# Windowed attention with a two-layer FFN, one core: the last six token chunks go through the first FFN product in pairs, by seven half-size products whose weights stream from a DRAM scratch

## The chip, the core and the metric

The kernel runs on one NeuronCore of a Trainium2 chip. Times are device microseconds (us) of one launch. TensorE is called PE (its weight loads PEld), VectorE DVE, ScalarE ACT, GpSimd POOL; SP is the queue that issues the DMAs.

## What is computed

Attention with 8 heads of width 64 over 8 sequences of 576 tokens, then, with the heads joined to 512 numbers per token, a feed-forward layer on the 4608 tokens; `window` is 32, `dilation` 4, `w_in` is 512 x 2048 and `w_out` 2048 x 512:

```python
scores = scale * np.matmul(q, k.transpose(0, 1, 3, 2))
mask_plain = (rel >= 0) & (rel < window)
mask_dil = (rel >= 0) & (rel < window * dilation) & (rel % dilation == 0)
masks = np.stack([mask_plain if h < H // 2 else mask_dil for h in range(H)], axis=0)
scores = np.where(masks[None, :, :, :], scores, -1000000000.0)
...
return np.matmul(attn, v).astype(np.float32)
...
h = x @ w_in
inv_sqrt2 = np.float32(1.0 / np.sqrt(2.0))
g = 0.5 * h * (1.0 + erf(h * inv_sqrt2))
return (g @ w_out).astype(np.float32)
```

## The kernel before, in words

The 4608 tokens are nine chunks of 512. Each operand of the FFN is split into a high and a low part of type fp32r, and a product of two such operands is three matmuls: high by high, low by high, high by low. One matmul is 128x128 weights by 512 tokens.

The feed-forward work of a chunk is 16 blocks `f` of 128 hidden units. For one `f`, `ffn_h` (line 551, matmuls at line 543) does 4 x 3 = 12 matmuls into one of PSUM's banks 4 and 5, ACT makes the GELU (line 557) and rounds it to the high part (line 560), and DVE subtracts to get the low part (line 562). `ffn_o` (line 564, matmuls at 567) then does 12 matmuls for the same `f` into the four output banks 0 to 3. So a chunk has 192 matmuls of the first product (h) and 192 of the second (o). Chunks 1 to 8 run them as eight h blocks, eight o blocks, eight h blocks and eight o blocks; in the last of these stages each output bank takes its 24 matmuls in one go and is copied out (line 585).

All 16 weight blocks stay in SBUF from chunk 0 on, as `weight` tiles of one pool, `wpool`, which has 19 buffers of 1 MB; the other three hold q, k and v as they arrive.

The attention of chunk n+1 is interleaved with the FFN of chunk n: scores (`scores`, line 372, 64 matmuls for two head pairs), the masked minimum (`lowest`, lines 406 and 412, DVE), the exponentials (`softmax`, line 420, ACT: eight per head pair), the reciprocal and the scaling (lines 429, 431, 445, DVE), the transposes (`turn`, lines 458 and 463, DVE), the product with v (`av`, line 507) and the split of its result into the x tiles (`xout`, lines 530 and 533).

Chunk 0, with the load and split of the weights and the attention of chunks 0 and 1, is laid out by a planner (`Plan`) with costs and ranks. From chunk 1 on the order is written by hand: each step gets a position in units of FFN blocks (`add`, `upto`), and is emitted when the FFN loop has come there. Every engine works its own instructions in the order of the program.

## Time and profile before

| | us |
|---|---|
| three timed runs, median | 896.36 |
| lowest and highest of them | 893.29, 896.65 |
| span of the profiled execution | 892.8 |
| PE busy in it | 878.7 |
| ACT busy | 387.2 |
| DVE busy | 354.0 |

The profile is of one further execution; its span runs from the first to the last instruction, and that is the time that its views divide up. A row of a group gives line, engine, operation, tiles and shape, the count, then busy time and the mean of one in ns, then the idle time in front of the group and what ended it. The chain of waits lists what the end of the span hung on, piece by piece, as start, length, engine and line. In the table of stretches each engine's busy time stands with its instruction count, then the granted TensorE clock as a share, the busy share of the 16 DMA engines and the GB/s.

### The profile page before, as it was taken

The numbers are of one execution on the slowest core, as the hardware profiler recorded it, in microseconds if no ns is written. First come the engines' busy times: TensorE is split into PE (matmuls) and PEld (weight loads), VectorE is DVE, ScalarE is ACT, GpSimd is POOL, SyncE is SP. The second block draws the span as 40 slices with busy tenths as digits, with TensorE's granted clock in tenths as the row PEclk, the third lists the DMA queues.
The fourth block names the chain that finished last, engine by engine and source line by source line (L and its number), as shares of the span: only waits on it lengthen the run. The fifth ranks groups of instructions, "written<-read, shape, count | busy, mean of one in ns | idle before, by whom it ended". The sixth has DMA issues, their size and how long they took to land.

```text
span 892.8 us, 19041 instructions
## 1 busy us (share of the span) xinstructions
PE 878.7 (98%) x8403; PEld 723.5 (81%) x8403; DVE 354.0 (40%) x594; ACT 387.2 (43%) x1028; POOL 11.6 (1%) x45
## 2 busy tenths in 40 slices
PE   6999999999999999999999999999999999999998
PEld 5778888888888888888888888888888888888886
DVE  6896963622254214621462136222542164212020
ACT  6886833733273325442354237332723263414040
POOL 5000000000000000000000000000000000000000
PEclk8899999999999999999999999999999999999999
DMA  9966124003300240004100330033002330010001
GB/s 373 415 253 235 48 95 143 1 1 119 120 1 1 68 150 23 0 1 173 65 1 1 131 107 1 1 119 120 1 1 72 126 124 0 1 38 12 1 1 47
DMA packets 16212, 71.20 MB, mean 80 GB/s; under 512 B 1794, under 2 KB 2050, under 8 KB 11650
## 3 DMA queue, kind: packets, MB, share of 16 engines
q1 hardware_dynamic: 16130, 70.00, 21.2%
q8 instruction: 65, 1.06, 0.5%
q14 instruction: 17, 0.14, 0.0%
HBM read 60.55 MB, written 9.44 MB: 78 GB/s over the span
## 4 chain that ended last, share of the span: by engine, by line
PE 95%; ACT 3%; DMA 1%; issue 1%; SPq 0%; DVE 0%; ACTq 0%
PE ps L567 44%; PE ps L543 43%; PE ps L507 3%; PE ps L372 3%; DMA raw_qk<-qk 1%; PE ps L486 1%; PE ps L719 1%; ACT sm L420 1%; PE ps L471 1%; PE ps L499 0%; ACT sm L442 0%; ACT raw_w L266 0%; ACT weight L297 0%; ACT L557 0%; ACT gf L557 0%
## 5 line engine op out<-in xcount | busy, mean ns | idle before, releaser
L567 PE MATMUL ps<-g,weight 128*128 128x512 f32 x1728 | 402.5, 391 | 0.5 <-DVE g L562 0.5
L543 PE MATMUL ps<-x,weight 128*128 128x512 f32 x1728 | 401.4, 390 | 0.0
L543 PEld LDWEIGHTS ps<-x,weight 128*128 128x128 f32 x1728 | 322.9, 188 | 68.0
L567 PEld LDWEIGHTS ps<-g,weight 128*128 128x128 f32 x1728 | 322.8, 188 | 68.2 <-DVE g L562 1.0
L562 DVE TENSOR_TENSOR g<-gf,g 128x512 fp32r<-128x512 f32 x144 | 99.6, 692 | 384.7 <-ACT g L560 384.7
L557 ACT ACTIVATE gf<-ps 128x512 f32<-128x512 f32 x144 | 86.2, 599 | 316.6 <-PE ps L543 316.6
L560 ACT CAST g<-gf 128x512 fp32r<-128x512 f32 x144 | 89.4, 621 | 4.6
L420 ACT ACTIVATE sm<-sm,st 128x64 f32<-128x64 f32 (+1 forms) x224 | 74.9, 337 | 0.1
L196 ACT COPY o_sb<-ps 128x512 f32<-128x512 f32 (+1 forms) x35 | 20.3, 581 | 108.7 <-PE ps L567 103.2
L533 DVE TENSOR_TENSOR x<-ps,x 128x512 fp32r<-128x512 f32 (+1 forms) x38 | 32.0, 847 | 88.4 <-ACT x L530 88.4
L530 ACT CAST x<-ps 128x512 fp32r<-128x512 f32 (+1 forms) x38 | 29.9, 798 | 64.0 <-PE ps L507 40.6
L463 DVE STREAM_TRANSPOSE turned<-sm 32x256 f32<-32x256 f32 x104 | 45.4, 436 | 2.0
L420 ACT ACTIVATION_READ_ACCUMULATOR sm<-sm,st 128x1 f32 x224 | 42.1, 188 | 0.0
L372 PEld LDWEIGHTS ps<-raw_qk 64*32 64x32 f32 x2304 | 25.0, 108 | 9.2 <-issue 5.2
L372 PE MATMUL ps<-raw_qk 64*32 64x64 f32 (+1 forms) x2304 | 28.8, 232 | 2.8 <-DMA raw_qk<-qk 2.7
L507 PEld LDWEIGHTS ps<-turned,v_sb 64*64 64x64 f32 x1664 | 25.4, 135 | 4.6 <-issue 4.6
L507 PE MATMUL ps<-turned,v_sb 64*64 64x32 f32 x1664 | 26.9, 220 | 0.0
L420 ACT ACTIVATE sm<-ps,st 128x64 f32<-128x64 f32 x64 | 19.0, 328 | 6.0 <-DVE st L431 3.6
L445 DVE TENSOR_TENSOR sm<-sm,st 128x512 f32<-128x512 f32 x30 | 20.8, 692 | 0.9
L292 DVE SCALAR_TENSOR_TENSOR weight<-raw_w,spare 128x1024 fp32r<-128x1024 uint32 x16 | 19.6, 1224 | 0.5
L286 DVE SCALAR_TENSOR_TENSOR raw_w<-raw_w,spare 128x1024 uint32<-128x1024 uint32 x16 | 19.5, 1218 | 0.1
L297 ACT CAST weight<-raw_w 128x1024 fp32r<-128x1024 f32 x16 | 18.5, 1156 | 1.2 <-DVE raw_w L286 1.2
(58 smaller groups left out, 269.5 us busy)
## 6 DMA issues: line engine op xcount, KB each, us to landing
v_sb<-v SPq DMA_DIRECT2D x17, 1024.0 KB, 5.2
raw_qk<-qk SPq DMA_DIRECT2D x32, 512.0 KB, 5.2
raw_w<-w SPq DMA_DIRECT2D x16, 1024.0 KB, 14.0
outT<-o_sb SPq DMA_DIRECT2D x35, 256.0 KB, 2.2
mid_w<-w SPq DMA_DIRECT2D x4, 1023.5 KB, 16.6
raw_qk<-qk_ld SPq DMA_DIRECT2D x2, 1024.0 KB, 7.0
v_wide<-v_ld SPq DMA_DIRECT2D x2, 768.0 KB, 5.6
raw_qk<-qk_lp SPq DMA_DIRECT2D x2, 640.0 KB, 4.0
```

Of the source, the lines that this page charges most:

```text
L372: nc.tensor.matmul(s.sc[32 * r:32 * r + 32, h, c0:c0 + s.nk], x[:, q0:q0 + 32], x[:, k0:k0 + s.nk], start=s.c > 1, stop=s.c > 1 or u == NU ...
L420: nc.scalar.activation(t, s.sc[:, i // NU, at:at + 2 * KB] if s.c < 2 else t, AF.Exp, bias=s.st[:, 0, i:i + 1], scale=SCALE if s.c < 2 els ...
L445: nc.vector.tensor_mul(s.all, s.all, t.unsqueeze(2).broadcast_to((P, 2 * NU, 2 * KB)))
L463: nc.vector.transpose(s.t[32 * to:32 * to + 32, :, r % 2], s.all[32 * r:32 * r + 32, :, j * KB:(j + 1) * KB])
L507: nc.tensor.matmul(px(r)[h * D:(h + 1) * D, u * KB:(u + 1) * KB], s.v[rows, u, j, h * D:(h + 1) * D], s.t[rows, h * NU + slot(s, u), j], s ...
L530: nc.scalar.copy(h, y)
L533: nc.vector.tensor_sub(l, y, h)
L543: nc.tensor.matmul(bank, weights[f][:, t, cc * P:(cc + 1) * P], x[:, xx], start=n == 0, stop=n == 3 * NC - 1)
L557: nc.scalar.activation(gf, bank, AF.Gelu)
L560: nc.scalar.copy(g[:, 0], gf)
L562: nc.vector.tensor_sub(g[:, 1], gf, g[:, 0])
L567: nc.tensor.matmul(ps[:, d], weights[f][:, t, DM + d * P:DM + (d + 1) * P], gs[f][:, u], start=f == 0 and n == 0, stop=f == NF - 1 and n == 2)
```

## The change

Chunk 0 stays as it is. Chunks 1 and 2 keep the direct product (`chunk`). Chunks 3 to 8 are taken as three pairs. For a pair, the 1024 tokens are cut into two halves of 512 (alternate runs of 32 tokens), the 512 inputs of the FFN into two halves of 256, and the 2048 hidden units into `f` and `f + 8`. The four quarter products of that 2x2 block form are got from seven products P1 to P7 of half size, each 6 matmuls for one `f` of 8 (`product`), and their sums. So the first product of a pair is 7 x 6 x 8 = 336 matmuls in place of 384. The second product stays direct, 2 x 192.

What that needs beside the matmuls:

- **Weights and sums of weights** (`prepare`, in chunk 1, eight times, one every 6.5 us of the plan): POOL adds high and low part of two weight blocks (2 x 512 columns), DVE makes four sums or differences, ACT and DVE split five of the results into high and low parts in the four slots of a tile `units`, and SP stores them in a DRAM scratch: five stores of 256 KB from `units` (line 817), two of 256 KB (lines 821, 822) and two of 512 KB (line 825) straight from the `weight` tiles. Eight times that is 72 stores.
- **Streaming back** (`fetch`, line 1070): the weight blocks leave SBUF in chunk 2; their buffers become a ring of six, two tiles of x (`late["x", ..]`) and eight tiles `c` that hold the four quarter products of one `f` in fp32. Per pair 8 + 8 + 16 blocks of 1 MB, 768 KB and 1 MB come through the ring.
- **Operands** (`operand`): sums of x halves on DVE, split by ACT and DVE into `xs` tiles, seven per pair of two tiles each, in place of the x tiles of `xout`; `put_x` (line 892) now only copies a chunk's x from PSUM.
- **Adding up**: per pair and `f` three copies from PSUM to `c` by ACT (`set_to`) and six adds of a PSUM bank to a part of `c` by DVE (`add_up`, line 1153).
- **GELU** on the sums in `c` in SBUF (line 1214), five blocks ahead of the second product (`LEAD`), where before it read PSUM.

All work from chunk 1 on stands in one list of events with planned times (0.2267 us for a matmul, `MM`), sorted; attention is planned by `duo` (two head pairs), uses PSUM banks 6 and 7 alone, and the other six banks are handed out in the order in which they were given back (`free`). A pair has three stages: x (P1, P2, P4, P7: 24 matmuls per `f`), z (P3, P5, P6: 18 per `f`), and the two second products (2 x 192). The attention of the next two chunks lies in them. `softmax` may now be interrupted between its eight exponentials. The host undoes the order of the tokens at the end.

The core of the diff:

```diff
-    for c in range(1, NCH):
-        for f in range(half):
-            at_once(ffn_h(c, f, gs))
-            upto(base + f + 1)
...
+    def prepare(t, f):
...
+        def sums(i):
+            def go():
+                st["p"] = have("prep", lambda: kept([P, 4, 2, NW1], F32, "prep"))
+                x = weights[f + HALF * i][:, :, 0:DM].bitcast(F32)
+                nc.gpsimd.tensor_add(st["p"][:, i].rearrange("p k n -> p (k n)"), x[:, 0], x[:, 1])
...
+        def unit(n, of, to):
+            def high():
+                q = have("units", lambda: kept([P, 4, 2, NW1], F32R, "units"))
+                nc.scalar.copy(q[:, n % 4, 0], st["p"][:, of[0], of[1]])
+            def low():
+                q = late["units"]
+                nc.vector.tensor_sub(q[:, n % 4, 1], st["p"][:, of[0], of[1]], q[:, n % 4, 0])
+            def put():
+                nc.sync.dma_start(to, late["units"][:, n % 4].bitcast(F32))
+        def plain():
+            nc.sync.dma_start(wx[f][:, P2], b(0).bitcast(F32))
+            nc.sync.dma_start(wz[f][:, P5], b(3).bitcast(F32))
+            for i in range(2):
+                g = f + HALF * i
+                nc.sync.dma_start(w2[g // 2][:, g % 2], weights[g][:, :, DM:].bitcast(F32))
+        ev(t - 2, 4, sums(0))
+        ev(t - .9, 4, sums(1))
+        ev(t - 1.2, 0, plain)
+        for n, (of, to) in enumerate(targets):
+            at = t + 1.1 * n
+            if n == 0 or first[n] != first[n - 1]:
+                ev(at, 4, both(first[n]))
+            high, low, put = unit(5 * f + n, of, to)
+            ev(at + .5, 4, high)
+            ev(at + 1, 4, low)
+            ev(at + 1.5, 0, put)
...
+        for f in range(HALF + 1):
+            w = lambda f=f: slab_w(first + f, 4)
+            if f < HALF:
+                t = unit(t, ops, ("x", P1), f, w)
+                ev(t, .5, set_to(f, X22, (("x", P1), f), True))
+                t = unit(t, ops, ("x", P4), f, w)
+                ev(t, .5, set_to(f, X21, (("x", P4), f)))
+            if f:
+                g = f - 1
+                t = unit(t, ops, ("x", P7), g, lambda g=g: slab_w(first + g, 4), on=(("x", P4), g))
+                ev(t, .5, add_up(g, X11, (("x", P4), g), base=X22, gives=True))
+                ev(t, .6, add_up(g, X22, (("x", P2), g), -1, gives=True))
+            if f < HALF:
+                t = unit(t, ops, ("x", P2), f, w)
+                ev(t, .5, add_up(f, X21, (("x", P2), f)))
...
+        for f in range(HALF + 1):
+            w = lambda f=f: slab_w(first + HALF + f, 3)
+            if f < HALF:
+                t = unit(t, opz, ("z", P3), f, w)
+                ev(t, .5, set_to(f, X12, (("z", P3), f)))
...
+            for f in range(NF):
+                ev(t + 12 * MM * (f - LEAD), 4, make(f))
+            begin = t
+            t = o_first(t, acc, range(NF - 4), gs, w_of)
+            t = o_last(t, acc, range(NF - 4, NF), gs, w_of, (3 + 2 * n + 1 - b) * N, end=n == NPAIRS - 1 and b == 1)
...
+    chunk(T1, 1, ((0, 8), (8, 16)))
+    chunk(T2, 2, ((0, 8), (8, 12), (12, 16)))
+    for f in range(HALF):
+        prepare(12 + 6.5 * f, f)
+    duo(2, 0, dict(v=[Q[0]]), dict(s=[3], e=[22.5, 27.5], n=33, v=[18], av=66))
+    duo(2, 2, dict(v=[Q[0]]), dict(s=[10], e=[32.5, 37.5], n=43, v=[69], av=76))
...
+    for n in range(NPAIRS):
+        t, at = two_chunks(tp[n], n)
+        if n == NPAIRS - 1:
+            break
...
+    for i in range(len(slabs)):
+        ev(done_at[i - RING] + .02 if i >= RING else T2 + 46 + i * 3, 0, fetch(i))
```

How the order on the engines changes, at three places. The first is PE. Before, in a chunk from 1 to 6 (`x,weight` is the first product, `g,weight` the second, `raw_qk` the scores, `turned,v_sb` the product with v):

```order
L543 MATMUL ps<-x,weight 128x512 x24
L372 MATMUL ps<-raw_qk 32x64 x64
L543 MATMUL ps<-x,weight 128x512 x24
L372 MATMUL ps<-raw_qk 32x64 x64
L543 MATMUL ps<-x,weight 128x512 x48
L567 MATMUL ps<-g,weight 128x512 x96
L543 MATMUL ps<-x,weight 128x512 x96
L567 MATMUL ps<-g,weight 128x512 x9
L507 MATMUL ps<-turned,v_sb 64x32 x64
L567 MATMUL ps<-g,weight 128x512 x24
L507 MATMUL ps<-turned,v_sb 64x32 x64
L567 MATMUL ps<-g,weight 128x512 x63
```

Now, in the first pair from the middle of stage x on (`xs,ring` is a half-size product, `g,ring` the second product, both with streamed weights; `qkv` holds q, k and v):

```order
L1121 MATMUL ps<-xs,ring 128x512 x60
L507 MATMUL ps<-turned,qkv 64x32 x64
L1121 MATMUL ps<-xs,ring 128x512 x24
L372 MATMUL ps<-qkv 32x64 x64
L1121 MATMUL ps<-xs,ring 128x512 x24
L507 MATMUL ps<-turned,qkv 64x32 x64
L1121 MATMUL ps<-xs,ring 128x512 x90
L998 MATMUL ps<-g,ring 128x512 x36
L507 MATMUL ps<-turned,qkv 64x32 x64
L998 MATMUL ps<-g,ring 128x512 x60
L507 MATMUL ps<-turned,qkv 64x32 x64
L998 MATMUL ps<-g,ring 128x512 x288
```

The attention matmuls are as many as before and sit between the products; every weight now comes from the ring.

The second place is ACT in the second h stage of chunk 1. Before, in the eight h blocks of a chunk that carry the exponentials of the next (`gf` is a GELU from PSUM, `g` its high part, `sm` the exponentials):

```order
L557 ACTIVATE gf<-ps 128x512
L560 CAST g<-gf 128x512
L420 ACT_TABLE_LOAD
L420 ACTIVATE sm,st<-sm,st 128x64 x32
L557 ACT_TABLE_LOAD
```

Now, at the last three GELUs of chunk 1 (`units` is the tile that the stores read):

```order
L810 CAST units<-prep 128x256 x2
L982 ACTIVATE gf<-ps 128x512
L992 CAST g<-gf 128x512
L810 CAST units<-prep 128x256 x3
L982 ACTIVATE gf<-ps 128x512
L992 CAST g<-gf 128x512
L982 ACTIVATE gf<-ps 128x512
L992 CAST g<-gf 128x512
L420 ACT_TABLE_LOAD
```

Casts into `units` now stand ahead of the GELUs, and each of them needs a slot whose store, four casts earlier, has landed.

The third place is DVE. Before, after the second h stage of a chunk has begun (the scaling and the transposes of the next chunk's attention):

```order
L562 TENSOR_TENSOR g<-gf,g 128x512 x2
L429 TENSOR_SCALAR st<-st 128x8
L431 RECIPROCAL st<-st 128x8
L445 TENSOR_TENSOR sm<-sm,st 128x512
L458 STREAM_TRANSPOSE turned<-sm 128x512
L463 STREAM_TRANSPOSE turned<-sm 32x8x32 x4
```

Now, towards the end of stage x of the first pair (`c<-c,ps` adds a PSUM bank to a quarter product):

```order
L429 TENSOR_SCALAR st<-st 128x8
L431 RECIPROCAL st<-st 128x8
L1153 TENSOR_TENSOR c<-c,ps 128x512 x2
L445 TENSOR_TENSOR sm<-sm,st 128x512
L458 STREAM_TRANSPOSE turned<-sm 128x512
L463 STREAM_TRANSPOSE turned<-sm 32x8x32 x2
L1153 TENSOR_TENSOR c<-c,ps 128x512 x2
L463 STREAM_TRANSPOSE turned<-sm 32x8x32 x2
L1153 TENSOR_TENSOR c<-c,ps 128x512 x3
L406 SCALAR_TENSOR_TENSOR sm<-ps,masks 128x512
```

The same attention steps now share DVE with the adds that give PSUM banks back to PE.

More of the change, by code (lines that the diff above doesn't have):

```diff
@@ L771, in attn_ffn @@
[L771 to L798 removed]
+    MM = 0.2267
@@ new lines, in drip, with kept, have @@
+    def drip(t, dt, n, rank, gen):
+        go = stepper(gen)
+        for i in range(n):
+            ev(t + i * dt, rank, go)
+    free = [4, 5, 0, 1, 2, 3]
+    def kept(shape, dtype, name):
+        return wpool.tile(shape, dtype, tag="w", name=name if isinstance(name, str) else name[0])
+    late = {}
+    def have(name, make):
+        if name not in late:
+            late[name] = make()
+        return late[name]
+    scratch = ctx.enter_context(tc.tile_pool(name="scratch", bufs=1, space=bass.MemoryType.DRAM))
@@ new lines, in h_unit, with mm, gelu @@
+    def h_unit(t, c, f, gs):
+        st = {}
+        def mm():
+            st["bank"] = free.pop(0)
+            bank, n = ps[:, st["bank"]], 0
+            for cc in range(NC):
+                x = xs[c][cc].x
+                for i, j in ((0, 0), (1, 0), (0, 1)):
+                    nc.tensor.matmul(bank, weights[f][:, i, cc * P:(cc + 1) * P], x[:, j], start=n == 0, stop=n == 3 * NC - 1)
+                    n += 1
+        def gelu():
+            st["gf"] = work.tile([P, N], F32, tag="go", name="gf", bufs=3)
+            nc.scalar.activation(st["gf"], ps[:, st["bank"]], AF.Gelu)
+            free.append(st["bank"])
+            split(gs, f, st["gf"])
+        end = t + 12 * MM
+        ev(t, 1, mm)
+        ev(end, .5, gelu)
+        return end
@@ new lines, in split, with o_part, o_first, mm @@
+    def split(gs, f, x):
+        g = gs[f] = xg.tile([P, 2, N], F32R, tag="xg", name="g")
+        nc.scalar.copy(g[:, 0], x)
+        nc.vector.tensor_sub(g[:, 1], x, g[:, 0])
+    def o_part(acc, d, f, g, w, first, last):
+        n = 0
+        for i, j in ((0, 0), (1, 0), (0, 1)):
+            nc.tensor.matmul(ps[:, acc[d]], w[:, i, d * P:(d + 1) * P], g[:, j], start=first and n == 0, stop=last and n == 2)
+            n += 1
+    def o_first(t, acc, fs, gs, w_of):
+        def mm(f):
+            def go():
+                if not acc:
+                    acc.extend(free[:NC])
+                    del free[:NC]
+                for d in range(NC):
+                    o_part(acc, d, f, gs[f], w_of(f), f == 0, f == NF - 1)
+            return go
+        for f in fs:
+            ev(t, 1, mm(f))
+            t += 12 * MM
+        return t
@@ new lines, in o_last, with mm, go, put @@
+    def o_last(t, acc, fs, gs, w_of, col, end=False):
+        def mm(d):
+            def go():
+                for f in fs:
+                    o_part(acc, d, f, gs[f], w_of(f), f == 0, f == NF - 1)
+            return go
+        def put(d, i, n):
+            def go():
+                if i == 0:
+                    gs["out", d] = work.tile([P, N], F32, tag="go", name="o_sb", bufs=3)
+                cols = slice(i * N // n, (i + 1) * N // n)
+                o = gs["out", d]
+                copy("DVE" if i else "ACT", o[:, cols], ps[:, acc[d], cols])
+                nc.sync.dma_start(outT[d * P:(d + 1) * P, col + cols.start:col + cols.stop], o[:, cols])
+                if i == n - 1:
+                    free.append(acc[d])
+            return go
+        for d in range(NC):
+            ev(t, 1, mm(d))
+            t += 3 * len(fs) * MM
+            n = 2 if end and d == NC - 1 else 1
+            for i in range(n):
+                ev(t, .5, put(d, i, n))
+        return t
@@ new lines, in chunk, with slab @@
+    def chunk(t, c, parts):
+        gs, acc = {}, []
+        w_of = lambda f: weights[f][:, :, DM:]
+        for n, (lo, hi) in enumerate(parts):
+            for f in range(lo, hi):
+                t = h_unit(t, c, f, gs)
+            if n < len(parts) - 1:
+                t = o_first(t, acc, range(lo, hi), gs, w_of)
+            else:
+                t = o_last(t, acc, range(lo, hi), gs, w_of, c * N)
+        return t
+    RING, QKV = 6, 3
+    slabs, used = [], []
+    def slab(src, width):
+        slabs.append((src, width))
+        return len(slabs) - 1
@@ L889 @@
     out = r.results[0]["outT"].T
-    parts = out[:B * N].reshape(B, N, DM), out[B * N:].reshape(B, REST, DM)
+    one, two = out[:3 * N].reshape(3, N, DM), out[3 * N:].reshape(3, 2, 2, 8, 32, DM)
+    two = two.transpose(0, 2, 3, 1, 4, 5).reshape(6, N, DM)
+    chunks = np.concatenate([one, two], 0)
+    parts = chunks[:B], chunks[B].reshape(B, REST, DM)
     return np.ascontiguousarray(np.concatenate(parts, 1).reshape(B * S, DM))
```

362 lines of the change are left out of this document (305 added, 57 removed).

## Prediction

> **What bounds the kernel now.** I read the page first: span, busy times, the chain by engine.
>
> ```profile
> span 892.8 us, 19041 instructions
> PE 878.7 (98%) x8403; PEld 723.5 (81%) x8403; DVE 354.0 (40%) x594; ACT 387.2 (43%) x1028; POOL 11.6 (1%) x45
> ...
> PE 95%; ACT 3%; DMA 1%; issue 1%; SPq 0%; DVE 0%; ACTq 0%
> ```
>
> PE is busy 98% of the span and carries 95% of the chain. A busy PE can still be a slow one, so the chain in order of time comes next, for the price of one matmul and for gaps.
>
> ```profile
> 135.35 5.44 PE ps L543 x24
> 140.79 1.41 PE ps L372 x91
> 142.20 5.67 PE ps L543 x24
> ...
> 160.39 21.76 PE ps L567 x96
> ...
> 255.17 21.76 PE ps L567 x96
> ...
> 300.73 2.00 PE ps L507 x128
> 302.72 5.67 PE ps L567 x24
> ...
> 889.26 0.03 ACTq L196
> ```
>
> Chunk 1 begins at 135.35; from there to 889.26 the chain holds nothing but PE. 96 matmuls take 21.76, so one takes 0.2267 us and a chunk's 384 take 87.05. A scores step costs 1.41, and 0.23 more in the 24 matmuls behind it (5.67 in place of 5.44): 1.64. A product with v costs 2.00 + 0.23 = 2.23. The same stage of chunks 1 and 2 begins at 160.39 and 255.17, so a chunk takes 94.78 = 87.05 + 2 x 1.64 + 2 x 2.23. PE has no gap. Third view, the stretch of one chunk:
>
> ```profile
> 371.00:458.00 87.00, 87.00 (x864) 71.87 (x863) 27.19 (x46) 37.13 (x105) 0.00 (x0) 1.00 0.18 62
> ```
>
> DVE works 27 and ACT 37 of 87 us, the clock is granted in full, DMA moves 62 GB/s. So from 135 us on the time is the count of matmuls, and the other engines have more than half their time to spare.
>
> **The change, part by part.** *Matmuls.* Three pairs lose 384 - 336 = 48 matmuls each: 144 x 0.2267 = 32.6 us off the path. Shape, clock and attention steps stay, chunk 0 (up to 135.35) and the 3.5 us of tail behind 889.26 too. Everything else that the change adds lies beside PE; what it costs is what PE must wait.
>
> *Preparing the weights, in chunk 1.* The rows for it, DMA first: the queue's packets, MB and share of the 16 engines in the first 40 us (loads) and in the last 133 us (stores of the result alone), then KB and landing times of single issues.
>
> ```profile
> q1 hardware_dynamic: 2630, 15.57, 95.9%
> q1 hardware_dynamic: 1296, 2.10, 4.3%
> outT<-o_sb SPq DMA_DIRECT2D x35, 256.0 KB, 2.2
> v_sb<-v SPq DMA_DIRECT2D x17, 1024.0 KB, 5.2
> raw_w<-w SPq DMA_DIRECT2D x10, 1024.0 KB, 17.3
> ```
>
> Loads ran at 15.57 MB / (0.959 x 40 us) = 406 GB/s, stores at 2.10 MB / (0.043 x 133 us) = 367 GB/s while they lasted. Each of the eight rounds stores 7 x 256 KB and 2 x 512 KB, 2.88 MB: 7.9 us at that price, where the plan gives a round 6.5. So the DMA engines are the limit there.
>
> When must it be done? PE reaches plan position 65.3, the end of the second h stage, 65.3 + 3 x 1.64 = 70.2 us after the chunk's start, and uses the last GELU block 4.8 us later, at 75. On ACT the last cast into `units` stands ahead of the last two GELUs.
>
> ```profile
> L562 DVE TENSOR_TENSOR g<-gf,g 128x512 fp32r<-128x512 f32 x144 | 99.6, 692 | 384.7 <-ACT g L560 384.7
> L557 ACT ACTIVATE gf<-ps 128x512 f32<-128x512 f32 x144 | 86.2, 599 | 316.6 <-PE ps L543 316.6
> L560 ACT CAST g<-gf 128x512 fp32r<-128x512 f32 x144 | 89.4, 621 | 4.6
> L196 ACT COPY o_sb<-ps 128x256 f32<-128x256 f32 x1 | 0.4, 372 | 4.9 <-PE ps L567 4.9
> L198 DVE COPY o_sb<-ps 128x256 f32<-128x256 f32 x1 | 0.4, 425 | 20.2 <-ACT o_sb L196 20.2
> ```
>
> Behind that cast follow 2 x (0.60 + 0.62) and 0.69, 3.1 us, so it must end by 71.9. It waits for the store four casts earlier. The first store can go out at about 17 (position 12 + 1.5, plus PE's 3.3 of attention by then). Up to the store waited for lie 23.07 MB, less the first 1.57 that need no sums, less the last four stores (1.05), plus one load of v (1.05): 21.5 MB / 367 GB/s = 58.6 us, and 1.5 for it to land: 77.1. PE loses 77.1 - 71.9 = 5.2 if the DMA engines never idle. They will, a little, since a slot's next store needs the landing, a cast (0.37) and a subtraction (0.43): for four short stops of half a microsecond I add 2 and take 7. Ends: nothing, if the engines run at the loads' 406 GB/s and the first stores leave with the chunk; 15, if DVE adds to it. In those 51 us of plan DVE has 40 subtractions behind the casts (17.0), 8 sums of full and 24 of half width (15.7), the minima, scaling and transposes of four head pairs (19.6, rows below) and 11 GELU subtractions (7.6): 59.9 us by row durations. But then
>
> ```profile
> 149.19 0.69 DVE L562 TENSOR_TENSOR g<-gf,g 128x512 fp32r<-128x512 f32 x1 [0.70 <-ACT g L560]
> 149.80 0.69 DVE L406 SCALAR_TENSOR_TENSOR sm<-ps,masks 128x512 f32<-128x512 f32 x1
> ```
>
> instructions that don't need each other follow at 0.61, which makes it 54. DVE too is full there.
>
> *Chunk 2.* Exponentials are planned among its first three GELUs, and each change of function costs a table load.
>
> ```profile
> 43.61 1.28 ACT L420
> 44.90 2.48 ACT sm L420 x16
> ```
>
> Seven loads (9.0), 16 exponentials at 0.31 and the rest are 17.3 us of ACT in 10.9: 6.4 late. All six banks are free for h then, 16.3 us of PE, so that is hidden; without that cover it would cost 6. The v tile of the second duo in chunk 1 may only be loaded when the first has been used, 24 matmuls (5.44) ahead of its own use, and v lands in 5.2: nothing, or up to 4 while stores still drain. I take 0 for both.
>
> *Streaming.* A pair loads 30 blocks' worth of 1 MB and up to 8 MB for attention, some 40 x 10^6 bytes in 178 us, 225 GB/s against 406; a block lands in 5.2 and PE takes 4.1 to 5.4 for one, with five more in the ring (over 20 us). Each fetch holds SP until PE has left a ring buffer, with q, k, v loads and result stores behind it; since all stand in the plan's order, they are late only by what PE is late. 0; if the cover went, each late block would cost PE its lateness.
>
> *Stages x and z.* Here DVE gives PE its banks back.
>
> ```profile
> L463 DVE STREAM_TRANSPOSE turned<-sm 32x256 f32<-32x256 f32 x104 | 45.4, 436 | 2.0
> L533 DVE TENSOR_TENSOR x<-ps,x 128x512 fp32r<-128x512 f32 x34 | 29.7, 875 | 71.5 <-ACT x L530 71.5
> L458 DVE STREAM_TRANSPOSE turned<-sm 128x512 f32<-128x512 f32 x26 | 18.5, 712 | 0.9
> L412 DVE TENSOR_REDUCE st<-sm 128x8 f32<-128x512 f32 x26 | 17.8, 686 | 0.9
> L406 DVE SCALAR_TENSOR_TENSOR sm<-ps,masks 128x512 f32<-128x512 f32 x24 | 16.4, 684 | 0.0
> L431 DVE RECIPROCAL st<-st 128x8 f32<-128x8 f32 x36 | 7.3, 202 | 1.3 <-ACT st L427 0.2
> L429 DVE TENSOR_SCALAR st<-st 128x8 f32<-128x8 f32 x32 | 5.5, 170 | 26.3 <-ACT sm L420 25.7
> ```
>
> The 48 adds from PSUM aren't in the trace: between 0.68 (L406, dense rows from PSUM) and 0.875 (L533, scattered rows); I take 0.69, since `c` is dense. That is 33.2; ten operand steps 6.9; eight head pairs at 0.684 + 0.686 + 0.170 + 0.202 + 0.692 + 0.712 + 4 x 0.436 = 4.89 (the scaling, L445, at the 0.692 of L562), less what falls behind stage z (5.3), 33.9; six GELU subtractions 4.2. Together 78.2 in 336 x 0.2267 + 4 x 1.64 + 2 x 2.23 = 87.2 us of PE: 90%. In the first pair DVE is 4 to 5 us behind when z ends, and the fourth output bank, given back by P5's last adds, allows 3.3: 1 us lost. In the second pair seven table loads fall among the first GELUs; ACT has 18.5 us of work in 11.7, 6.8 late, and P6 allows its copy of P3's bank 4.8: 2, and 1 for DVE. The third pair carries no attention: 0. In all 4.
>
> *Sum.* 892.8 - 32.6 + 7 + 0 + 0 + 4 = 871.2 of span. The median of the runs shown, 896.36, lies 3.6 above the profiled span; with the same 3.6, **874.8 us**. About 0.5% (4.5 us) is what a measurement of this kernel can tell from no change: faster is below 891.9, slower above 900.8.
>
> **The rivals.** *Nothing is lost.* The stores keep up and PE runs through: 896.4 - 32.6 = 863.8. For it: a cast that is late by a few us finds PE with two banks in hand. Against: 2.88 MB in 6.5 us is 443 GB/s, more than any stretch of the trace. Chance 0.15.
>
> *DVE is the bound of stages x and z.* With 0.875 for an add, 48 x 0.185 = 8.9 more, 87.1 of 87.2, and each wait for PE or ACT is then lost: some 7 in each of two pairs, 889. For it: the 90%. Against: the 0.61 spacing. Chance 0.13.
>
> *POOL and DVE take turns.* POOL's sums lie between two DVE sums of successive rounds.
>
> ```profile
> L213 POOL MEMSET masks<- 128x320 f32 x1 | 0.4, 364 | 0.0
> ```
>
> The trace's largest POOL instruction, 320 columns in 0.36 us, gives 0.58 for 512 by proportion, and up to twice that for two inputs. If DVE stands still for all 16 sums, 9 to 18 us join its 54, the chain ends some 10 later, and the time is 885. For it: nothing in this trace, where the two engines never share such work. Chance 0.08. The Trainium skill (SBUF — State Buffer, section on the two separate sides) says that a GpSimd instruction and a DVE instruction with two SBUF inputs hold a shared port pair for their whole length, and the other blocks; by that rule this case is the one that comes.
>
> *Slower: the stores run one behind the other.* Place: the 72 stores of chunk 1, four slots, SP in order, each landing waited for. Price: alone a 256 KB store takes 2.2 us to land, 119 GB/s; at half the 367, 184 GB/s, the 21.5 MB take 117 us, the last cast ends at 135, PE loses 63, and the time is 896.4 - 32.6 + 63 + 4 = 931. It makes the kernel slower when the rate is below about 250 GB/s (21.5 MB in 86 us: 33 lost here, 37 in all). For it: with a full queue a 1 MB load took 17.3 to land. Against: that queue still moved 406 GB/s, and eight DMAs may be on their way at once. Chance 0.14. The Trainium skill (DMA: Bandwidth & Descriptors, rules for kernel authors) asks for 1 MB and more per DMA for full bandwidth, which speaks against stores of 256 KB; the 367 GB/s of the row speak for them.
>
> **How the numbers follow.** My forecast (PE loses 5 to 20) has 0.50; with 0.15, 0.13, 0.08 and 0.14 that is 1. Low end 862, a little under the case without loss; high end 893, which takes in the DVE and POOL cases and leaves out the slower one. Faster: 0.50 + 0.15 + 0.08 and most of the DVE case, 0.80; same 0.06; slower 0.14.
>
> **What would show it.** Right: 3312 PE matmuls of 128x512 in the FFN at 0.2267; PE idle mostly in chunk 1, about 50 to 75 us into it, with ACT's casts into `units` waiting for a DMA; that stretch's DMA share near 1. Wrong: no wait of those casts (then 864); PE waiting for L1153 in every `f` (DVE bound); POOL instructions much over 1 us with DVE idle behind them; stores landing ever later (slower). A PE that waits for `ring` would be a case that I have left out.

## The result, and the profile after

The changed kernel takes 908.52 us (median of four runs, 908.31 to 910.89), the kernel before 895.88 in the same comparison (893.29 to 896.65): a ratio of 1.0152, 95% interval 1.0133 to 1.0171. It is 12.6 us slower. The prediction was 874.8, range 862 to 893: wrong, and on the wrong side. The profiled span is 906.8 against 892.8, 14.0 more.

The page of the changed kernel, with the rows that stood first in the prediction, and the granted clock in 40 slices:

```profile
span 906.8 us, 19643 instructions
PE 858.8 (95%) x8259; PEld 702.8 (78%) x8259; DVE 501.5 (55%) x856; ACT 468.9 (52%) x1202; POOL 33.4 (4%) x61
PEclk9899999978999999999999999999898999999999
...
PE 65%; ACT 6%; DVE 6%; issue 2%; POOL 1%; DVEq 0%; ACTq 0%; POOLq 0%
```

PE has 144 matmuls less and is busy 858.8 in place of 878.7 us, only 19.9 less where 144 matmuls are 32.6: the rest ran slower (the 7 and 8 in the clock's row). And 48 us of the span are now without PE work, where before there were 14. PE's share of the chain falls from 95 to 65%. What PE waits for, behind chunk 0:

```profile
PE ps L977 <- ACT gf L982: 20.8, 4, 16.5
PE ps L1121 <- ACT c L1160: 5.7, 1, 5.7
PE ps L499 <- issue: 4.3, 2, 2.8
...
PE ps L507 <- DVE sm L406: 1.6, 1, 1.6
```

Four rows, 32.4 us, nearly all of it in three places. Nothing waits for the ring. PE's own order in time gives the first instructions of chunk 1, chunk 2 and the three pairs (the last matmul of pair 3 ends at 903.2):

```profile
135.73 5.60 PE L977 MATMUL ps<-x,weight 128*128 128x512 f32 x24
...
257.23 1.48 PE L372 MATMUL ps<-qkv 64*32 64x64 f32 x128
...
363.07 1.52 PE L1121 MATMUL ps<-xs,ring 128*128 128x512 f32 x6
...
542.51 1.52 PE L1121 MATMUL ps<-xs,ring 128*128 128x512 f32 x6
...
739.85 5.38 PE L1121 MATMUL ps<-xs,ring 128*128 128x512 f32 x23
```

With 0.2267 for a matmul, 1.64 for a scores step and 2.23 for a product with v, as in the prediction, each part's work and loss. Pair 2's last steps have other sizes, so its loss is not measured by itself: it is what is left when the other parts are taken from the whole.

| part | work | measured | lost | forecast |
|---|---|---|---|---|
| chunk 1 | 87.05 + 3 x 1.64 + 2 x 2.23 = 96.4 | 121.5 | 25.1 | 7 |
| chunk 2 | 87.05 + 3 x 1.64 + 4 x 2.23 = 100.9 | 105.8 | 4.9 | 0 |
| pair 1 | 163.2 + 4 x 1.64 + 4 x 2.23 = 178.7 | 179.4 | 0.7 | 1 |
| pair 2 | 182.0 | 197.3 | 15.3 | 3 |
| pair 3 | 163.2 | 163.4 | 0.2 | 0 |

The whole is 46.2: the 14.0 between the two spans and the 32.6 of fewer matmuls, less 0.4 more in chunk 0. Of the 46.2 the waits are 33.9 (the four rows, and 1.5 in three more of at most 0.7). Of the other 12.3 some 10 are matmuls at half clock behind these waits: from 135 us on PE was busy for 19.6 us in which half its clock was granted. The stretch behind the stall of stage z in pair 2, from 632 us in pieces of 2 us (columns: engines' busy time, then granted clock, DMA share, GB/s):

```profile
632.00:634.00 2.00, 0.00 (x0) 0.00 (x0) 1.92 (x5) 1.97 (x3) 0.00 (x0) 0.69 0.79 332
...
636.00:638.00 2.00, 2.00 (x6) 1.54 (x6) 1.97 (x5) 1.97 (x4) 0.00 (x0) 0.50 0.00 0
...
640.00:642.00 2.00, 2.00 (x10) 1.62 (x10) 1.97 (x5) 0.00 (x0) 0.00 (x0) 1.00 0.96 401
```

PE begins again at 635.2 with half its clock and has all of it some 4 us later. Now the stall of 16.5 us in chunk 1: ACT's order there, and PE's first instruction behind it.

```profile
203.58 0.71 ACT L810 CAST units<-prep 128x256 fp32r<-128x256 f32 x2 [3.55 <-DVE prep L798]
204.31 1.28 ACT L982 ACT_TABLE_LOAD   x1
205.60 0.60 ACT L982 ACTIVATE gf<-ps 128x512 f32<-128x512 f32 x1
```

```profile
184.18 5.60 PE L977 MATMUL ps<-x,weight 128*128 128x512 f32 x24
206.25 4.52 PE L977 MATMUL ps<-x,weight 128*128 128x512 f32 x12 [16.47 <-ACT gf L982]
```

PE filled its two free banks by 189.8. The GELU that empties the first stands in ACT's order behind the casts of round 5 of the preparation, and those wait for that round's first sum on DVE (L798). So PE waits for as long as the rounds are late. DVE's first sum of each round began at

```profile
150.33 0.69 DVE L798 TENSOR_TENSOR prep<-prep 128x512 f32<-128x512 f32 x1
...
162.86 0.69 DVE L798 TENSOR_TENSOR prep<-prep 128x512 f32<-128x512 f32 x1 [0.58 <-POOL prep L791]
...
175.14 0.69 DVE L798 TENSOR_TENSOR prep<-prep 128x512 f32<-128x512 f32 x1
183.50 0.69 DVE L798 TENSOR_TENSOR prep<-prep 128x512 f32<-128x512 f32 x1 [1.18 <-POOL prep L791]
...
226.06 0.68 DVE L798 TENSOR_TENSOR prep<-prep 128x512 f32<-128x512 f32 x1
```

8.4 to 12.5 us apart where the plan has 6.5. What holds a round was the question of the experiments; who waited in 150 to 230 us:

```profile
ACT units L810 <- DVE prep L798: 15.3, 6, 3.6
DVE g L993 <- ACT g L992: 9.2, 9, 2.0
ACT units L810 <- DVE prep L800: 8.9, 4, 2.8
DVE units L814 <- ACT units L810: 8.6, 16, 1.6
...
ACT units L810 <- issue: 4.0, 2, 2.1
...
DVE prep L798 <- POOL prep L791: 2.7, 4, 1.2
```

The casts wait 30 us for sums on DVE (15.3, 8.9 and two smaller rows). No row of this run names a store; at most the 4.0 with no releaser in the trace can be waits for one.

### The profile page after: what moved, and what is told of

It is laid out like the page before. It is cut to its first block, busy times and chain, and to the rows that moved or that the text cites. A ratio compares the mean times of both kernels' runs of the same rounds, so it can differ in the third digit from the quotient of the medians.

```text
span 906.8 us, 19643 instructions
## 1 busy us (share of the span) xinstructions
PE 858.8 (95%) x8259; PEld 702.8 (78%) x8259; DVE 501.5 (55%) x856; ACT 468.9 (52%) x1202; POOL 33.4 (4%) x61
## 4 chain that ended last, share of the span: by engine, by line
PE 65%; ACT 6%; DVE 6%; issue 2%; POOL 1%; DVEq 0%; ACTq 0%; POOLq 0%
PE ps L998 36%; PE ps L1121 22%; PE ps L507 3%; PE ps L977 2%; PE ps L372 2%; ACT g L992 1%; ACT sm L420 1%; DVE turned L463 1%; DVE c L1153 1%; ACT gf L982 1%; ACT L420 1%; ACT L982 1%; DVE g L993 1%; POOL prep L791 1%; DVE sm L445 1%
## 5 line engine op out<-in xcount | busy, mean ns | idle before, releaser
L998 PE MATMUL ps<-g,ring 128*128 128x512 f32 x1152 | 266.7, 393 | 0.5 <-DVE c L1153 0.5
L998 PEld LDWEIGHTS ps<-g,ring 128*128 128x128 f32 x1152 | 218.3, 190 | 46.8 <-DVE c L1153 0.9
L1121 PE MATMUL ps<-xs,ring 128*128 128x512 f32 x1008 | 234.4, 392 | 5.7 <-ACT c L1160 5.7
L1121 PEld LDWEIGHTS ps<-xs,ring 128*128 128x128 f32 x1008 | 188.9, 189 | 46.0 <-ACT c L1160 6.1
L993 DVE TENSOR_TENSOR g<-c,g 128x512 fp32r<-128x512 f32 x96 | 66.1, 690 | 138.8 <-ACT g L992 138.7
L1153 DVE TENSOR_TENSOR c<-c,ps 128x512 f32<-128x512 f32 x144 | 96.0, 683 | 70.0 <-PE ps L1121 68.5
L977 PE MATMUL ps<-x,weight 128*128 128x512 f32 x384 | 93.7, 402 | 20.8 <-ACT gf L982 20.8
L977 PEld LDWEIGHTS ps<-x,weight 128*128 128x128 f32 x384 | 73.3, 193 | 38.5 <-ACT gf L982 22.7
L998 PE MATMUL ps<-g,weight 128*128 128x512 f32 x384 | 92.3, 397 | 0.7 <-ACT g L992 0.7
L998 PEld LDWEIGHTS ps<-g,weight 128*128 128x128 f32 x384 | 72.6, 191 | 17.4 <-ACT g L992 1.3
L993 DVE TENSOR_TENSOR g<-gf,g 128x512 fp32r<-128x512 f32 x32 | 23.1, 721 | 50.7 <-ACT g L992 50.5
L543 PE MATMUL ps<-x,weight 128*128 128x512 f32 x192 | 46.8, 393 | 0.0
L567 PE MATMUL ps<-g,weight 128*128 128x512 f32 x192 | 46.3, 391 | 0.5 <-DVE g L562 0.5
L567 PEld LDWEIGHTS ps<-g,weight 128*128 128x128 f32 x192 | 35.9, 188 | 8.3 <-DVE g L562 0.9
L543 PEld LDWEIGHTS ps<-x,weight 128*128 128x128 f32 x192 | 35.6, 188 | 7.6
```

The source lines that it names most:

```text
L543: nc.tensor.matmul(bank, weights[f][:, t, cc * P:(cc + 1) * P], x[:, xx], start=n == 0, stop=n == 3 * NC - 1)
L567: nc.tensor.matmul(ps[:, d], weights[f][:, t, DM + d * P:DM + (d + 1) * P], gs[f][:, u], start=f == 0 and n == 0, stop=f == NF - 1 and n == 2)
L977: nc.tensor.matmul(bank, weights[f][:, i, cc * P:(cc + 1) * P], x[:, j], start=n == 0, stop=n == 3 * NC - 1)
L993: nc.vector.tensor_sub(g[:, 1], x, g[:, 0])
L998: nc.tensor.matmul(ps[:, acc[d]], w[:, i, d * P:(d + 1) * P], g[:, j], start=first and n == 0, stop=last and n == 2)
L1121: nc.tensor.matmul(ps[:, bank()], w()[:, key, i, k * P:(k + 1) * P], ops[key][k][:, j], start=start and n == 0, stop=n == 5, skip_group_ch ...
```

## The experiments

All times are medians; "before" ran beside each (895.7 to 896.9). The parts are read from PE's order in the one profiled execution, as in the table above. Chunk 0 is the same in all these kernels and ended between 135.1 and 137.3, so a difference of 2 us between two single executions says little. Whether chunk 2 takes 104.3 or 105.8 in the runs without the three orders below hangs on where one wait falls in the steps of the clock, not on what an edit leaves out (last section).

| run | us | ratio to before, 95% interval | chunk 1 | chunk 2 |
|---|---|---|---|---|
| changed kernel | 908.5 | 1.0133 to 1.0171 | 121.5 | 105.8 |
| stores_once | 908.6 | 1.0117 to 1.0151 | 121.4 | 105.9 |
| sums_on_dve | 906.3 | 1.0089 to 1.0125 | 118.6 | 105.8 |
| rounds_10 | 901.5 | 1.0044 to 1.0074 | 108.6 | 111.2 |
| three_places | 892.9 | 0.9945 to 0.9975 | 121.5 | 102.6 |
| low_later | 908.7 | 1.0123 to 1.0165 | 123.7 | 104.3 |
| low_dve | 906.6 | 1.0091 to 1.0136 | 121.8 | 105.8 |
| later_once | 905.2 | 1.0085 to 1.0115 | 119.7 | 104.3 |
| later_once_dve | 905.6 | 1.0059 to 1.0116 | 115.9 | 107.4 |
| no_low | 897.7 | 1.0004 to 1.0032 | 112.9 | 104.3 |
| no_low_once | 897.5 | 0.9992 to 1.0012 | 110.3 | 105.9 |
| no_low_dve_once | 894.2 | 0.9962 to 0.9993 | 107.4 | 104.3 |
| no_rounds | 882.9 | 0.9830 to 0.9863 | 96.6 | 105.9 |
| no_rounds_three | 867.7 | 0.9660 to 0.9689 | 96.6 | 102.6 |
| best_a | 880.8 | 0.9808 to 0.9851 | 104.6 | 105.4 |
| best_b | 878.1 | 0.9785 to 0.9830 | 106.6 | 103.5 |
| best_c | 875.4 | 0.9753 to 0.9786 | 101.9 | 105.1 |
| best_d | 880.8 | 0.9801 to 0.9836 | 101.1 | 109.5 |

**Are the stores the limit, as predicted?** In `prepare`, and in the list of what the pairs load:

```diff
             def put():
-                nc.sync.dma_start(to, late["units"][:, n % 4].bitcast(F32))
+                if f == 0:
+                    nc.sync.dma_start(to, late["units"][:, n % 4].bitcast(F32))
...
         def plain():
+            if f:
+                return
...
-            slab(wx[f].rearrange("p m t k -> p (m t k)"), 8 * NW1)
+            slab(wx[0].rearrange("p m t k -> p (m t k)"), 8 * NW1)
```

(`wz` and `w2` likewise.)

> Only round 0 of the preparation is stored; the 63 stores of rounds 1 to 7 are left out, and every load of the pairs reads what round 0 stored, so all later products use round 0's weights. All sums, casts and subtractions are still made. Theory A (hand-overs between DVE, ACT and POOL set a round): chunk 1 stays within 4 us of its 121.5, the time 904 to 909. Theory B (the stores set the pace, as the prediction has it): the casts wait for nothing, chunk 1 falls to about 98, the time to about 884.

Without the stores the stretch from 150 to 230 us is the same but for the DMA share; first the changed kernel, then this run:

```profile
150.00:230.00 80.00, 59.20 (x364) 47.10 (x364) 60.41 (x120) 39.13 (x124) 19.06 (x14) 0.87 0.76 272
```

```profile
150.00:230.00 80.00, 59.49 (x403) 47.49 (x389) 60.15 (x119) 39.38 (x125) 19.05 (x14) 0.87 0.09 31
```

The DMA share falls from 0.76 to 0.09 and PE's busy time moves by 0.3 us. The stores are not what holds the rounds. The slower rival of the prediction, stores one behind the other, falls with this too. The rule of the Trainium skill that stood beside it (DMA: Bandwidth & Descriptors, rules for kernel authors: 1 MB and more per DMA) is not shown wrong by that, but it decides nothing here: taking 63 of the 72 stores away changed the time by 0.1 us.

**POOL's sums.**

```diff
-                nc.gpsimd.tensor_add(st["p"][:, i].rearrange("p k n -> p (k n)"), x[:, 0], x[:, 1])
+                nc.vector.tensor_add(st["p"][:, i].rearrange("p k n -> p (k n)"), x[:, 0], x[:, 1])
```

> The 16 full sums of the preparation go from POOL to DVE, nothing else changes. In the profile of the changed kernel chunk 1 takes 121.5 us (135.7 to 257.2) where its matmuls need 96.4, and the eight rounds begin 8.4 to 12.5 us apart in place of 6.5. Theory A, a chain of hand-overs: one tile holds the sums of a round, so POOL may begin the next round only behind DVE's last sum of this one, and takes 2.7 us for two sums while DVE's next sum waits; then DVE and ACT take turns. Two sums of some 0.65 us on DVE in place of 2.7 on POOL and two hand-overs of some 0.3 make a round about 2 us shorter: seven rounds, 14 us less, some 895 us. Theory B, the stores to DRAM set the pace: no change, 908. Theory C, DVE's own work is the limit: 16 x 0.65 = 10 us more on DVE, up to 918.

2.3 us less, not 14: POOL is a part, not the cause. Theory C, that 10 us more of work on DVE make it slower, fails here. The trace of the changed kernel shows what a sum on POOL costs beside its own time: POOL's two sums of round 4, and DVE at that moment.

```profile
190.09 2.67 POOL L791 TENSOR_TENSOR prep<-weight 128x512 f32<-128x512 f32 x2 [6.62 <-DVE prep L804]
```

```profile
190.46 1.18 DVE L814 TENSOR_TENSOR units<-prep,units 128x256 fp32r<-128x256 f32 x1
191.67 0.44 DVE L463 STREAM_TRANSPOSE turned<-sm 32x256 f32<-32x256 f32 x1
```

The subtraction takes 1.18 under the first sum; the transpose, with one input, runs in its 0.44 under the second. With the sums on DVE no L814 takes longer than 0.43. All 40 subtractions (from 130 to 245 us), in the changed kernel and in this run:

```profile
L814 DVE TENSOR_TENSOR units<-prep,units 128x256 fp32r<-128x256 f32 x40 | 22.0, 553 | 9.4 <-ACT units L810 9.1
L814 DVE TENSOR_TENSOR units<-prep,units 128x256 fp32r<-128x256 f32 x40 | 16.6, 418 | 8.9 <-ACT units L810 8.7
```

That is 5.4 us, and two other DVE instructions with two SBUF inputs lose 1.9 (L993 12.1 to 11.1, L445 3.6 to 2.7): DVE stood still for some 7.3 us under POOL's sums. That agrees with the page that the prediction cited (the Trainium skill, SBUF — State Buffer, section on the two separate sides): a DVE instruction with two SBUF inputs stands still while POOL holds the port. The rival of the prediction had 9 to 18 us for this: it did happen, a little under the low end. Since this run puts 10.9 us of sums on DVE in its place, it doesn't show what the standing still alone costs the kernel; DVE's work rises by the 3.6 that are left, and still 2.3 us are won.

**The turns of DVE and ACT.**

```diff
-            ev(at + 1, 4, low)
-            ev(at + 1.5, 0, put)
+            ev(at + 1.9, 4, low)
+            ev(at + 2, 0, put)
```

> In the preparation, each subtraction (DVE, behind ACT's cast of the same block) stands 0.9 us later in the plan, so that DVE makes the next block's sum while ACT casts this one; the work is the same. Where nothing else came between, a block took 1.28 us in the changed kernel (176 to 180 us: sum 0.42, cast 0.41, subtraction 0.43 by turns); five of them and the two sums on POOL make 9 to 10 us, a round as measured. The first run of sums on DVE took only 2 us off, the stores none. Theory A' (the turns between DVE and ACT within a round, five hand-overs each way, set its length): a block takes about 0.8, a round 2 to 2.5 us less, chunk 1 14 to 17 us less, some 892 to 895. Theory C (DVE's amount of work in this stretch): no change, 907 to 909.

Nothing. But the edit did not take the waits away: from 150 to 230 us DVE still waited 9.3 us for casts (8.6 before), in 8 waits in place of 16, and the casts now waited 11.1 us for stores. So this run alone decides nothing on the turns. Taken with the other two, so that two or all three of these limits are gone:

> The later subtractions, and also the 16 full sums on DVE in place of POOL. Theory A': with the turns gone, POOL's 2.7 us are what is left between two rounds, and taking them away gives 1 to 2 us a round more than the later subtractions alone, some 883 to 888. Theory C: DVE has 10 us more, so nothing more is won or it gets worse, 905 to 918.

> Later subtractions and only round 0 stored (the 63 stores of rounds 1 to 7 left out; all pairs read round 0's weights). Each edit by itself changed nothing (908.7 and 908.6 against 908.5). In the run of the later subtractions ACT's casts waited 11.1 us for stores where they waited some 4 before; so theory D: two limits of nearly the same length stand side by side, the turns of DVE and ACT (9 to 10 us a round) and the stores (2.88 MB at 315 to 337 GB/s, about 9), and each alone hides the other. Then both edits together win what neither wins alone: rounds of 7 to 8.5 us, chunk 1 10 us or more shorter, some 895 to 899. Theory C (DVE's amount of work, or POOL's sums between rounds): still no change, 906 to 909.

> As the run before, and the 16 full sums on DVE in place of POOL. If POOL's 2.7 us between two rounds are a third limit in the row (theory D), another 3 to 8 us are won, some 888 to 894. If DVE's amount of work is what is left (62 us busy in the 80 us from 150 to 230 with the sums on it), the time is the same as or worse than in the run before.

906.6, 905.2 and 905.6: none of the gains that theory D asked for. In the last of these DVE's waits for casts are down to 2.3 us, so there the turns are gone too, and chunk 1 is 5.6 us shorter. DVE itself is the row to look at, in the pieces of 10 us before and in PE's stall:

```profile
180.00:190.00 10.00, 10.00 (x46) 8.29 (x45) 9.29 (x23) 5.68 (x30) 0.00 (x0) 1.00 0.00 0
190.00:200.00 10.00, 0.81 (x4) 0.35 (x2) 9.71 (x23) 4.64 (x20) 0.00 (x0) 0.69 0.00 0
```

With no stores, no sums on POOL and hardly a turn, DVE is busy 9.3 and 9.7 of 10 us there. So the amount of its work came under test.

**DVE's amount of work.**

```diff
             def low():
+                if f:
+                    return
                 q = late["units"]
```

> The changed kernel with the subtractions of rounds 1 to 7 left out (35 DVE instructions of 0.42 us, 12 to 15 us; the stored low halves of those rounds are those of round 0, so the result is wrong); all casts, sums and stores are made. The turns go with them, but the run of the later subtractions showed that they are worth nothing by themselves. Theory C (DVE's amount of work in the stretch): chunk 1 loses 10 to 14 us less, some 895 to 898. Theory D (stores beside DVE): the casts then wait for stores, 2.88 MB a round at some 330 GB/s or about 9 us, and little is won: 903 to 908.

> The same, and the stores of rounds 1 to 7 left out too (all pairs read round 0's weights). Theory D: now neither DVE nor the stores hold a round, what is left is POOL's 2.7 us, the five sums and ACT's order, some 7 to 8 us a round: chunk 1 loses 8 us or less, some 889 to 893, and the gain over each run alone is more than the two gains added. Theory C alone: the same as the run before, within 2 us.

> Subtractions and stores of rounds 1 to 7 left out as before, and the 16 full sums on DVE in place of POOL. Chunk 1 took 110.3 us without subtractions and stores. If POOL's 2.7 us between two rounds are most of the 14 that are left, some 8 to 10 us are won: chunk 1 101 to 103, time 887 to 890. If it is the order of casts and sums against the GELUs in ACT's and DVE's queues, 2 to 3 at most, 894 to 896.

Theory C's time came true: 35 subtractions less, 14.5 us of DVE from 150 to 230 us (60.4 busy down to 46.0), make the kernel 10.9 us faster, 8.6 of it in chunk 1. The stores on top give nothing in time (897.5; 2.6 of chunk 1, with 1.6 of chunk 2 the other way), so theory D falls. POOL on top gives 3.3.

A subtraction is work, and it is also a turn between DVE and ACT. The pair of runs without that doubt is later_once_dve and no_low_dve_once: both are without the stores and without sums on POOL, and DVE waits for casts only 2.3 and 3.5 us. There the subtractions take chunk 1 from 115.9 to 107.4. So, by these single profiled executions, of the 25.1 us that chunk 1 loses, 5.6 go with turns, stores and POOL together, 8.5 with the subtractions, and 11 stay; that these are the order of what is left (casts and sums ahead of GELUs in two queues) is argued and was not split further.

**Without the preparation.** Rounds 1 to 7 not made at all, alone and with the three orders below:

```diff
+        if f:
+            return
         ev(t - 2, 4, sums(0))
```

> The changed kernel with rounds 1 to 7 of the preparation left out whole (sums, casts, subtractions, stores; all pairs read round 0's weights). If the preparation is the whole cause of chunk 1's loss, chunk 1 falls from 121.5 us to the 96.4 that its matmuls and attention steps need, and the time from 908.5 to 882 to 885. If something else in chunk 1 (attention of chunks 2 and 3 on DVE and ACT, the new order itself) takes a part, chunk 1 stays above 98 by that part.

> Rounds 1 to 7 left out whole, and the three changed orders of the earlier run (dense exponentials in chunk 2, late first GELUs, the last product with v in four parts). If the losses found are all there are, the products alone give what was counted for them: 896.4 - 32.6 = 864, with 2 to 4 us of small waits at the ends of stages z: 864 to 868. A time above 872 would mean that the seven products cost more than their matmuls.

Chunk 1 is 96.6 us, 0.2 over its work, and DVE's busy time in 150 to 230 us is 34.6 in place of 60.4. The preparation is the whole loss of chunk 1, the 11 us that stayed among it. With the three orders the kernel takes 867.7, 3.9 over the 863.8 that the count of matmuls gives: the losses found are all there are, and the seven products cost what their matmuls cost.

**Three orders behind chunk 1.**

```diff
-    duo(3, 2, dict(qk=[Q[0]], v=[Q[1]]), dict(qk=[79], s=[83], e=[T2 - 1, T2 + 4], n=T2 + 12, v=[T2 + 6], av=T2 + 36))
+    duo(3, 2, dict(qk=[Q[0]], v=[Q[1]]), dict(qk=[79], s=[83], e=[T2 - 1, T2 + 1.5], de=.31, n=T2 + 12, v=[T2 + 6], av=T2 + 36))
...
-                ev(t + 12 * MM * (f - LEAD), 4, make(f))
+                ev(t + 12 * MM * max(f - LEAD, -2), 4, make(f))
...
-                ev(at["av"] + 2 * i, 2, run(o))
-                ev(at["av"] + 2 * i + 2.5, 4, out(o))
+                ev(at["av"] + 6 * i, 2, run(o, 0))
+                ev(at["av"] + 6 * i + 3, 2, run(o, 2))
+                ev(at["av"] + 6 * i + 4.5, 4, out(o))
```

(`run(o, u)` makes the half of the product that begins at u.)

> Three orders changed behind chunk 1, no work added or removed. One: the 16 exponentials at the beginning of chunk 2 stand 0.31 us apart in the plan, so that fewer GELUs lie among them (chunk 2 loses 5 us now: PE waits for a product with v, and then runs at a lower clock). Two: the first GELUs of each o stage stand at most two blocks of matmuls ahead of it in place of five, behind the last exponentials (in pair 2 PE waits 5.7 us at the end of stage z for ACT, among seven table loads). Three: the four parts of the last product with v stand 3 us apart with other matmuls between them (PE now waits 4.3 us inside them for nothing that the trace shows). If table loads and the dense run of small matmuls are the causes: chunk 2 loses 1, pair 2 loses 2 to 4 in place of 15, time 892 to 896. Rival: DVE's backlog, not ACT, holds the end of stage z, and the last product waits for its v tile from DRAM; then both stalls stay and the time is 904 or more.

892.9, 15.6 less, as expected of the causes named. PE's waits in this run:

```profile
PE ps L977 <- ACT gf L982: 20.5, 4, 16.4
...
PE ps L1121 <- ACT c L1160: 1.7, 2, 1.2
...
PE ps L499 <- issue: 0.2, 1, 0.2
```

The 16.4 of chunk 1 stay. Stage z loses 1.2 in place of 5.7, the last product 0.2 in place of 4.3, the 1.6 of chunk 2 are gone, and so are the slow matmuls behind each: chunk 2 is 3.2 us shorter, pair 2 184.5 in place of 197.3. In the changed kernel ACT did this at the end of stage z in pair 2:

```profile
626.76 0.56 ACT L1160 COPY c<-ps 128x512 f32<-128x512 f32 x1
627.34 1.28 ACT L1214 ACT_TABLE_LOAD   x1
...
629.94 1.28 ACT L420 ACT_TABLE_LOAD   x1
...
632.06 1.28 ACT L1214 ACT_TABLE_LOAD   x1
...
634.54 0.58 ACT L1160 COPY c<-ps 128x512 f32<-128x512 f32 x1
```

The copy at 634.5 frees what PE waits for; three of the seven table loads stand between it and the copy before.

**More time for a round.** Only the spacing:

```diff
-        prepare(12 + 6.5 * f, f)
+        prepare(12 + 10 * f, f)
```

> The eight rounds are planned 10 us apart in place of 6.5, so the last one ends in chunk 2. Theories A and B: the rounds have the time that they were seen to take (8.4 to 12.5), so chunk 1 loses 0 to 5 us in place of 25, of which chunk 2 may give a few back; some 885 to 890 us. Theory C, that ACT and DVE have too much work in chunks 1 and 2 together: the loss moves into chunk 2, time above 900.

Chunk 1 gains 12.9 us and chunk 2 gives 5.4 back, among its exponentials and table loads: 7 of the 20 expected. All helpful edits together, first with the sums on POOL, then on DVE, then `prepare(3 + 11 * f, f)` and `prepare(3 + 12 * f, f)`:

> All that has helped by itself, with the sums on POOL: rounds 10 us apart, later subtractions, exponentials of chunk 2 dense, first GELUs of a stage at most two blocks ahead, the last product with v in four parts. If the losses are those found (chunk 1 25 us, chunk 2 5, pair 2 15 of which 13 are gone in the run of the three places), 893 - 15 to 22 = 871 to 878; the case without loss is 864. If what is taken from chunk 1 comes back in chunk 2, as in the run with rounds 10 us apart (7 won where 20 were to be had), some 880.

> The same with the 16 full sums on DVE. Theory A': equal to the variant on POOL within 2 us, since at 10 us a round POOL has time. Theory C (DVE's amount of work): slower than that one by some 5 us.

> All helpful edits with the sums on DVE, and the rounds planned from 3 us into chunk 1 on, 11 us apart (before: from 12 on, 10 apart). In the run with 10 apart chunk 1 still lost some 8 to 10 us in its second h stage, where casts stand ahead of GELUs in ACT's order. Theory: with the rounds earlier and farther apart each is done when it is due; 2 to 6 us less than that run's 878, so 872 to 876. Rival: DVE and ACT are in one order with PE's GELUs, so any round beside an h stage costs PE some us wherever it stands; then 878 to 882.

> The fastest variant so far (875.4), with the rounds 12 us apart in place of 11, from 3 us into chunk 1. Chunk 1 lost some 5 us there and chunk 2 some 2.6. If a round beside an h stage is late because of too little time: 1 to 3 us less, 872 to 874. If the order itself costs it (casts ahead of GELUs): the same, 875 to 877.

best_a came out as its second forecast had it (880). best_c is the fastest: 875.4, ratio 0.977 (0.9753 to 0.9786) to the kernel before, 2.3% faster than that and 3.6% than the changed kernel. Theory C's guess for best_b was wrong: with time enough, DVE takes the sums at no loss. At 12 us a round chunk 2 loses again: PE there waits 4.4 us for q and k. SP's queue in that place, and what SP waited for:

```profile
244.10 6.46 SPq L817 DMA_DIRECT2D wx<-units  x2
256.81 0.81 SPq L857 DMA_DIRECT2D qkv<-qk  x2
```

```profile
SPq L817 <- DVE units L814: 8.1, 4, 5.8
SPq L857 <- DVE units L814: 6.2, 1, 6.2
```

The load of q and k stands behind two stores in SP's order, and the preparation's subtractions on DVE release both: late rounds now hold up a load. The 5 us of chunk 1 and the 4 of chunk 2 that best_c still loses were not pursued.

## Why the prediction was wrong

- **Matmuls, 32.6 us off the path: right.** no_rounds_three is 867.7, within 4 us of the 863.8 of "nothing is lost".
- **Preparing the weights: the step that failed.** "So the DMA engines are the limit there" was the step, and the 7 us came out of the stores' rate. Without stores nothing changes. The limit that the runs show stood in the same paragraph, "DVE too is full there", 54 us of work in 51, and was given no price but the upper end of 15. Its size was about right: from the first sum on DVE to the last subtraction (150.3 to 233.9) DVE was busy 61.9 us, of which it stood still 7.3 under POOL's sums. But the sum took this work as a block that runs without gaps. It took 83.6 us and not 51, because in program order DVE waits for ACT's casts (8.6 us), for the rounding of GELUs (9.2) and for POOL's sums (2.7), and ACT's GELUs in turn stand behind casts that wait for DVE. PE's stall is that lateness: 25.1 in place of 7. The runs show 8.5 of it as DVE's subtractions and 5.6 as turns, stores and POOL together; the split of the other 11, which leave with the whole preparation, stays open.
- **POOL's sum** was put at 0.58 to 1.16 us by proportion from a memset; it takes 1.30 (median of 16). The Trainium skill (GPSIMD Engine Reference) has a measured add of 2048 elements with two inputs at 4497 ns, an estimate of 1.1 for 512 by proportion: near the upper end, and too short as well.
- **Chunk 2, 0 in place of 4.9.** The h banks did hide ACT's lateness, as the prediction said; no h matmul waited. What was overlooked is who else stands behind a late GELU: DVE's subtraction for it, then the readings of scores behind that on DVE (L406), then PE's product with v. That was 1.6 us of wait, 1.6 of slower matmuls behind it (24 in 7.32 us in place of 5.74) and 0.7 of another wait; 1.0 is not accounted for.
- **Stages x and z.** The adds: 0.683 each, forecast 0.69, and pair 1 lost 0.7, forecast 1: right, and the rival of DVE as bound of these stages falls. Pair 2: "3" where 15.3 were lost. The mechanism (seven table loads among the first GELUs) was right and three_places showed it. Its size was not: PE waited 5.7 where 2 were given, and ran slowly behind it.
- **Attention steps "stay".** This failed for the last product with v: 384 small matmuls nearly in one run lost 4.3 us inside, where the kernel before had them in four parts of 96 with other matmuls between.
- **No price for a stall's clock.** "The clock is granted in full" held for a kernel without stalls. Behind the longer stalls here (1.6 us and more) PE ran for 19.6 us at half clock, which is some 10 us lost, nearly as much as the whole loss that I forecast (11); behind the one of 1.3 us the clock stayed whole.
- **Streaming at 0: right.** Nothing waited for the ring, at 209 GB/s of mean traffic from 363 to 903 us.
- **The signs given beforehand.** PE idle in chunk 1 with casts waiting came true, but the casts waited for DVE (30 us), not for a DMA: the sign spoke against my step, and the stretch ended 92 us into the chunk, not 75. The slower rival had the sign of the result and another cause. The rival of POOL and DVE had a part of the cause, a DVE chain that ends late (7.3 us of standing still), and not its size; no rival had the waits of the two queues for one another.

## What to carry to other kernels

Work that is "free" because its engine is half idle over the span still has to fit its stretch: add up that stretch's queue, and then add the waits that its program order has inside it, since here DVE and ACT, which hand work to one another, took 83.6 us for 62 us of DVE's work. When several limits look alike, taking one away and seeing nothing proves nothing for the others; take away the amount of work on each engine in turn, and last all of it, which gives the ceiling. And a stall of PE can cost its length plus the slow matmuls behind it.
